# Preparing the experts' weights one matrix to a stretch, and counting taken tokens in f16

## The chip, the cores and the metric

One core of a Trainium2 chip runs the kernel. The time is that of the device for one execution, in microseconds, median over runs. The core's engines work side by side, each through its own instructions in order: PE (TensorE, with its weight loads shown as PEld), DVE (VectorE), ACT (ScalarE), POOL (GpSimd) and SP (SyncE, which here only starts transfers).

## The reference

Attention over 8 batches, 8 heads, 576 tokens, then a gated product of matrices, then a mixture of 8 experts in which every token goes to one expert. Scores are walked from the highest down, and an expert takes at most 576 tokens:

```python
logits = x @ w_gate
order = np.argsort(-logits.flatten())
for idx in order:
    tok, e = (int(idx) // E, int(idx) % E)
    if assigned[tok] >= 0 or counts[e] >= cap:
        continue
    assigned[tok] = e
    counts[e] += 1
for e in range(E):
    mask = assigned == e
    h = np.maximum(x[mask] @ w1[e], 0.0)
    out[mask] = h @ w2[e]
```

There are 4608 tokens of 512 values; `w1[e]` is 512 x 1024 and `w2[e]` is 1024 x 512, 2 MB each.

## The kernel before

The program goes through attention and the first matrices (to about 800 us), then a routing stage (about 857 to 1104 us), and then the experts, to the end.

**Routing.** `phase()` runs seven times, and in each it finds a threshold for every expert digit by digit, in nine levels: 63 levels in all. A level is a chain between PE and DVE. PE multiplies one-hot digits `T` with the masks `M` (p1, nine matmuls, L806); DVE makes `mk` (L821); PE sums it (p2, four matmuls, L827); DVE compares with the room left `R` to make `fl` (L830); PE sums `fl` with a constant matrix `q16` (p3, L832); DVE takes `dl` (L834), the mask `eq` (L840) and the next `M` (L789). Between p1 and `mk`, `taken` lowers `R` by the tokens that the level before has given out: a matmul of a constant `q32` with the counts `cnt`, both f32 (L796, shown as two instructions), and a subtraction on DVE (L797). Into the gaps of the chain `fill` puts a counted number of matmuls of another product: 2.4 behind p1, 2.2 behind p2, 5.2 behind p3. These come from `stream()`, which computes the rows of x (`px`, L966, 24 matmuls of 128x512 for each of 36 blocks) from `W34` and `g`; `g` is loaded by SP, split by ACT and corrected by an accumulating transfer of POOL (`gl`). PE, POOL and ACT are in hand-written order here; DVE's is the scheduler's.

**Preparing a weight matrix.** Each of the 16 matrices (`a` is `w1[e]`, `b` is `w2[e]`) is loaded by SP into a staging tile `esa` or `esb`, one buffer each (L1019); ACT takes the sums of squares in eight `red` steps (L1026, each with a read of the sum); `fin` adds them up on PE (L1031) and DVE makes a power of two from it; then eight `conv` steps write the scaled matrix as two f16 parts, the high one on ACT (L1040), the low one on DVE (L1041), into `ewa` or `ewb` (two buffers each). The ops of 0a, 0b and 1a (the number is the expert) are in the list `ew0`, from which `stream()` takes some after each block from its sixth on (L970 to L972). The converts of 0b and 1a are left out of that list and kept in `owed_w`.

**Experts.** They go in pairs, 0 to 3. A pair has four stretches: layer 1 of its first expert (units of 12 matmuls, L1121; ACT and DVE make `h`, L1123 and L1124), layer 2 on token blocks 0 to 3 (24 matmuls each, L1138; ACT makes `y`, L1141; POOL scatters it, L1143), layer 1 of the second expert, layer 2 on blocks 4 to 8. All of PE's results go through one psum pool `pe` of eight buffers. A unit is 128 or 192 tokens wide for expert 0 and 288 wide for the others. `gather(p)` fetches the tokens of a pair in nine blocks: an indirect transfer on POOL (L1092), a scale on DVE (L78 to L81), `x16` on ACT and DVE (L1096, L1097), a transposing transfer on SP (L1098). `interleave(a, b)` spreads the list b among the units of a; the scheduler may still move an instruction ahead where its inputs allow. Here b was: in layer 1 of the first expert, the second half of the second expert's weights (for pair 0 the converts in `owed_w`) in the first half of the units, and four gather blocks in the second; in blocks 0 to 3 the next pair's first `a` (in pair 0 after all of 1b); in layer 1 of the second expert five gather blocks; in blocks 5 to 8 the next pair's first `b` and second `a`.

Of the kernel before, what the change touches and what calls it, by code (L numbers as in the profile page):

```python
# [7 lines left out]
F32 = mybir.dt.float32  # L8
F32R = mybir.dt.float32r
F16 = mybir.dt.float16  # L10
BF16 = mybir.dt.bfloat16
I32 = mybir.dt.int32
AF = mybir.ActivationFunctionType
ALU = mybir.AluOpType
AX = mybir.AxisListType
# [6 lines left out]
DM, FF, E = 512, 1024, 8  # L22
# [23 lines left out]
def interleave(a, b):  # L46
    na, nb = len(a), len(b)
    ib = 0
    for ia, f in enumerate(a):
        f()  # L50
        while ib < nb and (ib + 1) * na <= (ia + 1) * nb:
            b[ib]()
            ib += 1
    while ib < nb:
        b[ib]()
        ib += 1
# [3 lines left out]
def moe_kernel(ctx, tc, q, k, v, moe_w1, moe_w2, moe_w3, moe_w_out, w_gate, ew1, ew2, out):  # L60
    nc = tc.nc
    P = 128
# [7 lines left out]
    ones = const.tile([P, P], F32, name="ones")  # L70
# [4 lines left out]
    def pow2(pool, m, name, TB=TB, **kw):  # L75
        n = m.shape[-1]
        t = pool.tile([P, 3, n], I32, name=name, **kw)
        nc.vector.tensor_scalar(t[:, 0], m.bitcast(I32), 24, 23, op0=ALU.logical_shift_right,  # L78
                                op1=ALU.logical_shift_left)
        nc.vector.tensor_scalar(t[:, 1], t[:, 0], -1.0, float((189 + TB) << 23), op0=ALU.mult, op1=ALU.add)  # L80
        nc.vector.tensor_scalar(t[:, 2], t[:, 0], float((65 - TB) << 23), None, op0=ALU.add)  # L81
        return t[:, 1].bitcast(F32), t[:, 2].bitcast(F32)
# [504 lines left out]
    for n, m in WSTEP.items():  # L587
        for _ in range(m):
            x = next(ws)
# [8 lines left out]
    for f in range(8):  # L598
        a, b_ = S3 + int(R3 * f), S3 + int(R3 * f + R3 / 2)
# [21 lines left out]
    first = {n0: g for g, (n0, n1) in enumerate(GROUPS)}  # L621
# [65 lines left out]
    nc.vector.tensor_copy(pf, pi)  # L687
    ones16 = rt.tile([P, P], F16, name="ones16")
    nc.gpsimd.memset(ones16, 1.0)
    q32 = rt.tile([P, P], F32, name="q32")  # L690
    nc.gpsimd.memset(q32, 0.25)
    ci = const_tile([P, P], F32, "ci", [[1, P]], 0, 0)
    ci4i = rt.tile([P, P], I32, name="ci4i")
    nc.gpsimd.iota(ci4i, pattern=[[1, P]], base=0, channel_multiplier=0)
# [52 lines left out]
    def phase():  # L747
# [45 lines left out]

        def taken(c):
            p4 = cwp["pr"].tile([P, E], F32, name="p4")
            nc.tensor.matmul(p4, q32, c, start=True, stop=True)  # L796
            nc.vector.tensor_tensor(out=R, in0=R, in1=p4, op=ALU.subtract)  # L797

        eq, A, owe = un, None, None
        for l in range(NL):  # L800
# [39 lines left out]
                nc.vector.scalar_tensor_tensor(eqn, d, dl, eq, op0=ALU.is_equal, op1=ALU.mult)  # L840
                Mn = M_of(eqn)
            with tc.issue_after(om[0].ins) if not last else ExitStack():
                cnt = rw.tile([P, E], F32, name="cnt")
                nc.vector.scalar_tensor_tensor(cnt, thr[:, 1 if last else 0], dl, p2, op0=ALU.is_equal, op1=ALU.mult)
                if l + 1 < 7 and TH < 9:
                    T_of(l + 1, TH, 9)
                nc.vector.scalar_tensor_tensor(ab, d, dl, eq, op0=ALU.is_ge if last else ALU.is_gt, op1=ALU.mult)
                if A is None:
                    A = ab
                    A_ = rw.tile(E36, F16, name="A")  # L850
                    nc.vector.tensor_copy(A_, ab)
                    A = A_
                else:
                    nc.vector.tensor_tensor(out=A, in0=A, in1=ab, op=ALU.add)
# [148 lines left out]
    EW = {}  # L1003
    ew0 = []
    cwp = {}

    owed_w = []

    def expert_w(e, part, width, early, late=False):
        nonlocal owed_w  # L1010
        cw = cwp["p"]
        ops = []
        for n, src, A_, N_, T in ((("a", ew1, 4, FF, 10), ("b", ew2, 8, DM, 15))[part],):
            k_ = 4096 // width
            d = {}

            def load(n=n, src=src, A_=A_, N_=N_, d=d):
                d["st"] = cw.tile([P, A_, N_], F32, name="es" + n)
                nc.sync.dma_start(d["st"], src[e].rearrange("(c p) f -> p c f", p=P))  # L1019
                d["m"] = cw.tile([P, 8], F32, name="em" + n, bufs=2)  # L1020
                d["w"] = cw.tile([P, 2, A_, N_], F16, name="ew" + n, bufs=2)
                d["s"] = d["st"].rearrange("p c f -> p (c f)")
                d["v"] = d["w"].rearrange("p z c f -> p z (c f)")

            def red(i, d=d):
                nc.scalar.activation(d["v"][:, 1, i * width:(i + 1) * width], d["s"][:, i * width:(i + 1) * width], AF.Square,  # L1026
                                     accum_out=d["m"][:, i:i + 1])

            def fin(n=n, T=T, d=d, k_=k_):
                m2 = cwp["ps"].tile([P, 512], F32, name="pe")  # L1030
                nc.tensor.matmul(m2[:, :k_], ones, d["m"][:, :k_], start=True, stop=True)  # L1031
                m3 = cw.tile([P, 1], F32, name="er" + n, bufs=2)
                nc.vector.tensor_reduce(m3, m2[:, :k_], axis=AX.X, op=ALU.add)
                d["sc"], i = pow2(cw, m3, "ep" + n, T, bufs=2)
                EW[e, n] = d["w"], i

            def conv(i, d=d):
                x = slice(i * width, (i + 1) * width)
                w, hi, lo = d["s"][:, x], d["v"][:, 0, x], d["v"][:, 1, x]
                nc.scalar.activation(hi, w, AF.Copy, scale=d["sc"])  # L1040
                nc.vector.scalar_tensor_tensor(lo, w, d["sc"], hi, op0=ALU.mult, op1=ALU.subtract)  # L1041

            ops.append(load)
            ops += [lambda i=i, f=red: f(i) for i in range(k_)]
            if early:
                ops += [lambda: None] * 3
            ops.append(fin)
            ops += [lambda i=i, f=conv: f(i) for i in range(k_)]
            if late:
                owed_w += ops[-k_:]  # L1050
                ops = ops[:-k_]
        return ops

    load_w34()
    prep_g(0)
# [8 lines left out]
    cwp["pr"] = pb.enter_context(tc.tile_pool(name="pr2", bufs=1, space=PSUM, reuse_waits="tile"))  # L1064
    cwp["ps"] = pb.enter_context(tc.tile_pool(name="pt", bufs=1, space=PSUM, reuse_waits="tile"))
    cwp["p"] = ctx.enter_context(tc.tile_pool(name="cw", bufs=1, side="right", reuse_waits="tile"))
    for x in range(3):
        ew0 += expert_w(x // 2, x % 2, 512, True, x > 0)
    ew0.pop(0)()

    with tc.manual_schedule(engines={mybir.EngineType.PE, mybir.EngineType.Pool, mybir.EngineType.Activation}):
        route()
# [73 lines left out]
            tc.declare_no_dep(d.ins, o.ins, reason="rows of other tokens")  # L1146
        scat.append(d)

    def weights(e, part):
        if (e, part) == (1, 1):  # L1150
            return owed_w
        return expert_w(e, part, 512, True) if 2 <= e < E else []

    for f in gather(0):
        f()
    for p_ in range(E // 2):
        e = 2 * p_
        more = gather(p_ + 1) if p_ + 1 < E // 2 else []
        first = [((0, P),), ((P, P),), ((2 * P, P),), ((3 * P, CAP - 3 * P),)]
        halves = [((0, 288), (288, 288))]  # L1160
        units = list(layer1(e, first if e == 0 else halves))
        interleave(units[:len(units) // 2], weights(e + 1, 1))
        interleave(units[len(units) // 2:], more[:4])
        interleave([lambda k_=k_: layer2(p_, k_) for k_ in range(4)],
                   (expert_w(1, 1, 512, True) if e == 0 else []) + weights(e + 2, 0))
        interleave(list(layer1(e + 1, halves)), more[4:])
        layer2(p_, 4)
        interleave([lambda k_=k_: layer2(p_, k_) for k_ in range(5, 9)], weights(e + 2, 1) + weights(e + 3, 0))


_INS = ['q', 'k', 'v', 'moe_w1', 'moe_w2', 'moe_w3', 'moe_w_out', 'moe2_w_gate', 'moe2_w1', 'moe2_w2']
# [33 lines left out]
```

## Time and profile before

| what | value |
|---|---|
| runs | 1553.21, 1556.84, 1563.21 us (median 1556.84) |
| profiled execution | 1554.94 us, span 1553.2 us |
| PE busy | 1370.7 us (88%) |
| PE weight loads | 933.2 us (60%) |
| DVE busy | 987.8 us (64%) |
| ACT busy | 947.5 us (61%) |
| POOL busy | 118.6 us (8%) |
| mean transfer rate | 167 GB/s |

Busy times are shares of the span of one execution. A matmul's duration in a row overlaps that of the next, so the distance of two starts tells what a matmul costs PE. A wait is the idle time of an engine just ahead of an instruction, put down to what came last.

### The profile page before, as it was taken

Reading aid. Unit: us, or ns where it says so; the run is one execution under the profiler, and the core shown is the slowest. Engines: PE = TensorE matmul, PEld = TensorE weight load, DVE = VectorE, ACT = ScalarE, POOL = GpSimd, SP = SyncE. Lnnn points to the kernel's source line nnn. Section 1 sums busy time; section 2 is a strip of 40 time slices with the busy share of each in tenths; the row PEclk is TensorE's granted clock in tenths of the full one; section 3 lists DMA queues with packets and bytes.
Section 4 is the critical chain, followed back from the end, with each engine's and each line's share of the span. In section 5 each row is a group of like instructions: output and inputs, shape, how many; then the busy total and the mean of one; then the engine's idle time right before and its main releaser. Section 6 shows DMA issues by size and latency. Waiting matters only on the chain. (4 is left out here: it accounts for less than half of the span.)

```text
span 1553.2 us, 32385 instructions
## 1 busy us (share of the span) xinstructions
PE 1370.7 (88%) x12622; PEld 933.2 (60%) x12622; DVE 987.8 (64%) x2986; ACT 947.5 (61%) x2213; POOL 118.6 (8%) x137
## 2 busy tenths in 40 slices
PE   4457887989899999989899999999589889899897
PEld 2335655666666666656567666666476456566663
DVE  8888989868987888785111777777666533632510
ACT  8879887767877777755233444664246754845521
POOL 0000000000000000010000110101142300110001
PEclk9667999999999999999999999999789989999999
DMA  7767896888767775649995877877395833621100
GB/s 260 175 160 180 188 239 147 170 157 180 209 150 187 174 163 124 120 97 261 270 298 140 247 195 204 197 192 178 119 220 185 204 122 102 184 95 62 68 28 35
DMA packets 385417, 259.52 MB, mean 167 GB/s; under 512 B 261872, under 2 KB 345328, under 8 KB 384240
## 3 DMA queue, kind: packets, MB, share of 16 engines
q1 hardware_dynamic: 372064, 215.47, 55.1%
q0 software_dynamic: 11520, 39.87, 11.0%
q8 instruction: 99, 1.62, 0.4%
q10 hardware_dynamic: 1680, 2.11, 0.4%
q14 instruction: 54, 0.44, 0.1%
HBM read 132.61 MB, written 39.86 MB: 111 GB/s over the span
## 5 line engine op out<-in xcount | busy, mean ns | idle before, releaser
L325 PE MATMUL ab<-xT,w1h 128*128 128x288 f16 x1536 | 222.5, 295 | 12.7 <-ACT a_sb L330 9.3
L325 PE MATMUL ab<-xT,w2h 128*128 128x288 f16 x1536 | 221.0, 294 | 3.8 <-DVE g L335 2.3
L1121 PE MATMUL pe<-xT,ewa 128*128 128x288 f16 (+2 forms) x1728 | 201.6, 282 | 14.9 <-DMA xT<-x 12.3
L1121 PEld LDWEIGHTS <-ewa 128*128 128x128 f16 x1728 | 162.6, 102 | 52.9 <-issue 15.2
L1138 PE MATMUL pe<-ewb,h 128*128 128x512 f16 (+1 forms) x960 | 189.1, 379 | 0.0
L325 PEld LDWEIGHTS <-w1h 128*128 128x128 f16 x1536 | 147.4, 101 | 64.6 <-issue 21.7
L245 ACT ACTIVATE E<-S,nb,cc 128x128 f32<-128x128 f32 (+4 forms) x288 | 181.5, 638 | 2.8 <-DVE P L256 1.0
L325 PEld LDWEIGHTS <-w2h 128*128 128x128 f16 x1536 | 148.5, 100 | 57.0 <-issue 14.0
L256 DVE SCALAR_TENSOR_TENSOR P<-E,rr,P 128x512 f16<-128x512 f32 (+4 forms) x288 | 156.0, 573 | 10.5 <-ACT P L255 10.1
L1138 PEld LDWEIGHTS <-h 128*128 128x128 f16 (+1 forms) x960 | 85.4, 101 | 99.1 <-issue 2.6
L300 PE MATMUL PV<-PT,v 128*64 128x128 f16 (+1 forms) x2880 | 100.9, 222 | 48.4 <-DMA PT<-P 28.3
L1124 DVE SCALAR_TENSOR_TENSOR h<-pe,h 128x288 f16<-128x288 f32 (+2 forms) x144 | 58.9, 420 | 113.3 <-ACT h L1123 113.3
L300 PEld LDWEIGHTS <-v 128*64 128x64 f16 x2880 | 83.8, 117 | 73.4 <-issue 35.6
L335 DVE SCALAR_TENSOR_TENSOR g<-ab,vr,a_sb 128x288 f32<-128x288 f32 x124 | 63.4, 512 | 99.3 <-PE ab L325 84.5
L966 PE MATMUL px<-W34h,gl 128*128 128x512 f32 x288 | 120.2, 418 | 1.3 <-DMA gl<-g 1.3
L966 PE MATMUL px<-W34h,gh 128*128 128x512 f32 x288 | 120.9, 420 | 0.0
L966 PE MATMUL px<-W34l,gh 128*128 128x512 f32 x288 | 120.4, 418 | 0.0
L255 ACT ACTIVATE P<-E,rr 128x128 f16<-128x128 f32 (+3 forms) x176 | 97.3, 604 | 22.9 <-DVE rr L249 13.6
L237 DVE TENSOR_REDUCE nb<-S 128x2 f32<-128x1024 f32 (+3 forms) x128 | 101.5, 813 | 5.1 <-PE S L228 5.0
L1123 ACT ACTIVATE h<-pe 128x288 f16<-128x288 f32 (+2 forms) x144 | 51.5, 378 | 87.0 <-PE pe L1121 87.0
L330 ACT ACTIVATE a_sb<-ab 128x288 f32<-128x288 f32 x128 | 52.1, 407 | 71.6 <-PE ab L325 71.5
L224 PE MATMUL S<-qkT 64*128 64x512 f16 (+3 forms) x768 | 78.6, 317 | 12.6 <-ACT E L245 12.6
(285 smaller groups left out, 2199.9 us busy)
## 6 DMA issues: line engine op xcount, KB each, us to landing
g<-gd SPq DMA_DIRECT2D x36, 512.0 KB, 5.1
gl<-g POOLq DMA_DIRECT2D x36, 512.0 KB, 6.1
gd<-g SPq DMA_DIRECT2D x62, 288.0 KB, 3.3
g<-gd SPq DMA_DIRECT2D x15, 1152.0 KB, 8.0
raw<-in_moe_w_dram SPq DMA_DIRECT2D x32, 512.0 KB, 4.4
esa<-in_moe_w_dram SPq DMA_DIRECT2D x8, 2048.0 KB, 8.9
esb<-in_moe_w_dram SPq DMA_DIRECT2D x8, 2048.0 KB, 9.4
v<-in_v_dram SPq DMA_DIRECT2D x8, 1280.0 KB, 6.3
```

The costliest lines, as they stand in the source:

```text
L224: nc.tensor.matmul(ps[:, hh, o:o + N], tq[r, a, m * P:m * P + P], tk[r, b, :N], start=a + b == 0, stop=False)
L237: nc.vector.tensor_reduce(nb[:, 0, k_:k_ + 2], ps[:, :, o:o + N], axis=AX.X, op=ALU.max)
L245: nc.scalar.activation(ef[:, a], pf_[:, a], AF.Exp, bias=nb[:, 1, x:x + 1], scale=c[:, 0:1], accum_out=sums[:, x:x + 1])
L255: nc.scalar.activation(hi, ef[:, at[x]], AF.Copy, scale=r[:, 1, x:x + 1])
L256: nc.vector.scalar_tensor_tensor(lo, ef[:, at[x]], r[:, 1, x:x + 1], hi, op0=ALU.mult, op1=ALU.subtract)
L300: nc.tensor.matmul(ps[hh * 64:hh * 64 + 64, c0:c0 + w], vt[:, zv, hh, j, :], s, start=z == 0 and j == 0, stop=z == 2 and j == nj - 1)
L325: nc.tensor.matmul(p[:, :288], w[:, zw, cc, :], x[:, zx, cc, c0:c0 + 288], start=first, stop=cc == 3 and zw == 1)
L335: nc.vector.scalar_tensor_tensor(g, ps["w2"][:, :288], iv[b][:, f:f + 1], a, op0=ALU.mult, op1=ALU.mult)
L966: nc.tensor.matmul(p, gh[a][:, f], W34[b][:, f], start=f == 0 and a + b == 0, stop=f == 7 and a == 1)
L1121: nc.tensor.matmul(p[:, :n], w1[:, a, cc, f * P:(f + 1) * P], t[:, 4 * b + cc, x], start=cc == 0 and a + b == 0, stop=cc == 3 and a == 1)
L1124: nc.vector.scalar_tensor_tensor(h[:, 1, f, x], p[:, :n], 0.0, h[:, 0, f, x], op0=ALU.max, op1=ALU.subtract)
L1138: nc.tensor.matmul(p[r0:r1], h[:, a, f, k_ * P + r0:k_ * P + r1], EW[e, "b"][0][:, b, f], start=f == 0 and a + b == 0, stop=f == 7 and a == 1)
```

## The change

The counts `cnt` are written in f16, and `taken` multiplies them with `q16`, the f16 constant that p3 uses already; `q32` and its memset go. Each matrix x = 2e + part is now a pair of a load and a list of ops in `mats`, and `phase_of(x, units, rows)` deals one matrix to one stretch: the load of the next matrix, x + 1, then the ops of matrix x, with the gather blocks put in at even distances, all spread over the stretch's units. Pair p's four stretches prepare the second expert's a and b, and the next pair's first a and b; gather blocks go 3, 2, 3 and 1 to the four. In the routing stage both loads of expert 0 are issued ahead, and `ew0` holds the ops of 0a, the load of 1a, and all ops of 0b with its converts.

```diff
-            nc.tensor.matmul(p4, q32, c, start=True, stop=True)
+            nc.tensor.matmul(p4, q16, c, start=True, stop=True)
...
-                cnt = rw.tile([P, E], F32, name="cnt")
+                cnt = rw.tile([P, E], F16, name="cnt")
...
-    owed_w = []
-
-    def expert_w(e, part, width, early, late=False):
...
+    def expert_w(e, part):
+        cw = cwp["p"]
+        n, src, A_, N_, T = (("a", ew1, 4, FF, 10), ("b", ew2, 8, DM, 15))[part]
+        width, k_ = 512, 8
+        d = {}
+
+        def load():
+            d["st"] = cw.tile([P, A_, N_], F32, name="es" + n)
+            nc.sync.dma_start(d["st"], src[e].rearrange("(c p) f -> p c f", p=P))
+
+        def red(i):
+            if i == 0:
+                d["m"] = cw.tile([P, 8], F32, name="em" + n, bufs=2)
+                d["w"] = cw.tile([P, 2, A_, N_], F16, name="ew" + n, bufs=2)
...
+        return load, ([lambda i=i: red(i) for i in range(k_)] + [lambda: None] * 3 + [fin]
+                      + [lambda i=i: conv(i) for i in range(k_)])
+
+    mats = [(lambda: None, [])] * (2 * E + 3)
...
-    for x in range(3):
-        ew0 += expert_w(x // 2, x % 2, 512, True, x > 0)
-    ew0.pop(0)()
+    for x in range(2 * E):
+        mats[x] = expert_w(x // 2, x % 2)
+    mats[0][0]()
+    mats[1][0]()
+    ew0 += mats[0][1] + [mats[2][0]] + mats[1][1]
...
-    def weights(e, part):
-        if (e, part) == (1, 1):
-            return owed_w
-        return expert_w(e, part, 512, True) if 2 <= e < E else []
+    def phase_of(x, units, rows):
+        load, ops = mats[x + 1][0], mats[x][1]
+        ops = [load] + ops
+        for i, f in enumerate(rows):
+            ops.insert((2 * i + 1) * len(ops) // (2 * len(rows)), f)
+        interleave(units, ops)
...
-        units = list(layer1(e, first if e == 0 else halves))
-        interleave(units[:len(units) // 2], weights(e + 1, 1))
-        interleave(units[len(units) // 2:], more[:4])
-        interleave([lambda k_=k_: layer2(p_, k_) for k_ in range(4)],
-                   (expert_w(1, 1, 512, True) if e == 0 else []) + weights(e + 2, 0))
-        interleave(list(layer1(e + 1, halves)), more[4:])
-        layer2(p_, 4)
-        interleave([lambda k_=k_: layer2(p_, k_) for k_ in range(5, 9)], weights(e + 2, 1) + weights(e + 3, 0))
+        phase_of(2 * e + 2, list(layer1(e, first if e == 0 else halves)), more[:3])
+        phase_of(2 * e + 3, [lambda k_=k_: layer2(p_, k_) for k_ in range(4)], more[3:5])
+        phase_of(2 * e + 4, list(layer1(e + 1, halves)), more[5:8])
+        phase_of(2 * e + 5, [lambda k_=k_: layer2(p_, k_) for k_ in range(4, 9)], more[8:])
```

DVE in the routing stage, at the converts of 0b, before the change (`ewb` is written by the low half of a convert; `mk`, `fl`, `dl`, `eq`, `M` are the level's chain):

```order
L1041 SCALAR_TENSOR_TENSOR ewb<-esb,epb,ewb 128x512
L821 TENSOR_TENSOR mk<-p_15260,delta 128x32
L721 TENSOR_TENSOR T<-dp,iok 128x640
L797 TENSOR_TENSOR R<-R,p_15270 128x8
L1041 SCALAR_TENSOR_TENSOR ewb<-esb,epb,ewb 128x512 x2
L830 SCALAR_TENSOR_TENSOR fl<-R,p_15279 128x8
L1041 SCALAR_TENSOR_TENSOR ewb<-esb,epb,ewb 128x512 x2
L834 TENSOR_REDUCE dl<-p_15288 128x1
L1041 SCALAR_TENSOR_TENSOR ewb<-esb,epb,ewb 128x512 x2
L840 SCALAR_TENSOR_TENSOR eq<-dp,dl,eq 128x36
L1041 SCALAR_TENSOR_TENSOR ewb<-esb,epb,ewb 128x512
L789 TENSOR_TENSOR M<-oh,eq 128x288
```

The same place after the change:

```order
L819 TENSOR_TENSOR mk<-p_15691,delta 128x32
L795 TENSOR_TENSOR R<-R,p_15701 128x8
L719 TENSOR_TENSOR T<-dp,iok 128x640
L1036 SCALAR_TENSOR_TENSOR ewb<-esb,epb,ewb 128x512
L828 SCALAR_TENSOR_TENSOR fl<-R,p_15711 128x8
L832 TENSOR_REDUCE dl<-p_15720 128x1
L838 SCALAR_TENSOR_TENSOR eq<-dp,dl,eq 128x36
L787 TENSOR_TENSOR M<-oh,eq 128x288
```

The eight converts stood in one level and R behind T; now there is one in a level, and R stands ahead of T.

ACT at the start of pair 1, before (`h` is layer 1's result; `ewb,emb<-esb` is a red of a b matrix, the wide rows are converts):

```order
L1123 ACTIVATE h<-pe 128x288 x2
L1026 ACTIVATE ewb,emb<-esb 128x512 x5
L1123 ACTIVATE h<-pe 128x288
L1026 ACTIVATE ewb,emb<-esb 128x512
L1123 ACTIVATE h<-pe 128x288
L1026 ACTIVATE ewb,emb<-esb 128x512 x2
L1123 ACTIVATE h<-pe 128x288
L1040 ACTIVATE ewb<-esb,epb 128x512 x8
```

After, at the same place (x_ rows are gather blocks):

```order
L1132 ACTIVATE y<-pe,s_16878 128x512
L1114 ACTIVATE h<-pe 128x288
L1087 ACTIVATE x_19399<-xg,xsc 128x512
L1114 ACTIVATE h<-pe 128x288 x2
L1087 ACTIVATE x_19512<-xg,xsc 128x512
L1114 ACTIVATE h<-pe 128x288 x3
L1021 ACTIVATE ewb,emb<-esb 128x512 x8
L1114 ACTIVATE h<-pe 128x288 x5
L1035 ACTIVATE ewa<-esa,epa 128x512 x8
L1114 ACTIVATE h<-pe 128x288 x5
```

The reds of a b matrix stood behind two units, and its fin on PE behind five; now they stand behind six units, and the convert among the units is that of an a matrix, whose reds ran earlier.

DVE in layer 1 of expert 0 (`xsc` and `x_` rows are gather blocks), before:

```order
L1097 SCALAR_TENSOR_TENSOR x_17691<-xg,xsc,x_17691 128x512
L1099 COPY sc<-xsc 128x1
L1124 SCALAR_TENSOR_TENSOR h<-pe,h 128x128
L1097 SCALAR_TENSOR_TENSOR x_17747<-xg,xsc,x_17747 128x512
L1124 SCALAR_TENSOR_TENSOR h<-pe,h 128x128
L78 TENSOR_SCALAR xsc<-xg 128x1
L1124 SCALAR_TENSOR_TENSOR h<-pe,h 128x192
L80 TENSOR_SCALAR xsc<-xsc 128x1
```

After, about the same place:

```order
L1036 SCALAR_TENSOR_TENSOR ewa<-esa,epa,ewa 128x512
L1090 COPY sc<-xsc 128x1
L1036 SCALAR_TENSOR_TENSOR ewa<-esa,epa,ewa 128x512
L78 TENSOR_SCALAR xsc<-xg 128x1
L1036 SCALAR_TENSOR_TENSOR ewa<-esa,epa,ewa 128x512
L1115 SCALAR_TENSOR_TENSOR h<-pe,h 128x128
L1036 SCALAR_TENSOR_TENSOR ewa<-esa,epa,ewa 128x512
L80 TENSOR_SCALAR xsc<-xsc 128x1
L81 TENSOR_SCALAR xsc<-xsc 128x1
L1036 SCALAR_TENSOR_TENSOR ewa<-esa,epa,ewa 128x512
L1088 SCALAR_TENSOR_TENSOR x_17657<-xg,xsc,x_17657 128x512
L1090 COPY sc<-xsc 128x1
```

The low halves of 1a's converts now stand among the `h` of this stretch; before there were none.

## Rows read from the trace of the kernel before

**Rows 1.** Windows of the trace: stretch, us, busy (instructions) of PE, PEld, DVE, ACT, POOL, clock, DMA share, GB/s

```profile
857.00:1104.00 247.00, 236.29 (x1738) 164.56 (x1737) 179.50 (x819) 125.85 (x237) 25.86 (x30) 0.98 0.78 199
1128.60:1158.70 30.10, 27.36 (x384) 27.27 (x385) 19.66 (x94) 14.72 (x42) 13.72 (x13) 0.88 1.15 218
1229.70:1339.90 110.20, 97.30 (x636) 61.03 (x635) 48.01 (x122) 62.14 (x145) 14.22 (x14) 0.94 0.46 136
1339.90:1442.10 102.20, 97.50 (x636) 61.09 (x635) 38.90 (x84) 57.67 (x137) 9.04 (x9) 0.97 0.30 106
```

**Rows 2.** Timeline of PE in routing: start us, us, engine, line, operation, count.

```profile
1060.49 0.39 PE L806 MATMUL p<-M,Tc 128*128 128x32 f16 x9
1060.73 0.37 PE L796 MATMUL p<-cnt,q 128*128 128x8 f32 x2
1060.95 0.48 PE L966 MATMUL px<-W34h,gl 128*128 128x512 f32 x1
...
1062.39 0.18 PE L832 MATMUL p<-fl,q 128*128 128x8 f16 x1
1062.43 0.47 PE L966 MATMUL px<-W34l,gh 128*128 128x512 f32 x1
...
1063.67 0.28 PE L796 MATMUL p<-cnt,q 128*128 128x8 f32 x2
1063.80 0.47 PE L966 MATMUL px<-W34h,gh 128*128 128x512 f32 x1
```

**Rows 3.** Windows of PE's px matmuls (L966) alone: stretch, us, busy (count), clock, DMA.

```profile
970.00:1005.00 35.00, 31.74 (x115) 1.00 0.81 193
1006.16:1014.51 8.35, 4.02 (x10) 0.80 0.66 168
1087.88:1098.42 10.54, 6.40 (x15) 0.68 0.51 143
```

**Rows 4.** Timeline of PE in the first clump of converts; in brackets idle before, releaser.

```profile
1008.06 0.24 PE L827 MATMUL p<-mk,selk 128*128 128x8 f16 x4 [1.50 <-DVE mk L821]
...
1013.71 0.29 PE L806 MATMUL p<-M,T 128*128 128x32 f16 x5 [0.84 <-DVE M L789]
```

**Rows 5.** Waits of DVE, 857 to 1104: us in total, times, longest.

```profile
DVE dl L834 <- PE p L832: 25.8, 56, 0.7
DVE fl L830 <- PE p L827: 24.3, 51, 2.3
```

**Rows 6.** Waits of PE, 870 to 960: the same columns.

```profile
PE p L806 <- DVE M L789: 1.9, 3, 0.8
PE px L966 <- DMA gl<-g: 1.3, 1, 1.3
```

**Rows 7.** Waits of PE in the experts, 1128 to 1554.

```profile
PE pe L1031 <- ACT ewb L1026: 22.1, 3, 12.9
...
PE pe L1121 <- DVE h L1124: 2.7, 1, 2.7
```

**Rows 8.** Timeline of PE at the end of pair 0 and starts of pairs 1 and 3.

```profile
1219.19 10.52 PE L1138 MATMUL pe<-ewb,h 128*128 128x512 f16 x48
...
1229.69 7.51 PE L1121 MATMUL pe<-xT,ewa 128*128 128x288 f16 x60
...
1250.55 18.73 PE L1121 MATMUL pe<-xT,ewa 128*128 128x288 f16 x132
...
1454.57 19.11 PE L1121 MATMUL pe<-xT,ewa 128*128 128x288 f16 x132
```

**Rows 9.** Timeline of SP's queue and ACT at the start of pair 1.

```profile
1232.66 0.37 SPq L1019 DMA_DIRECT2D esb<-in_moe_w_dram  x1
...
1244.46 0.63 ACT L1026 ACTIVATE ewb<-esb 128x512 f16<-128x512 f32 x1 [4.41 <-DMA esb<-in_moe_w_dram]
```

**Rows 10.** Tile esb (and ewb): operation, count, ns min/median/max; landing of its loads.

```profile
L1041 DVE SCALAR_TENSOR_TENSOR ewb<-esb,epb,ewb x64: 734/746/761, 1007.2 to 1460.7; 128x512 f16<-128x512 f32 x64
...
DMA to landing us min/median/max: 8.6/9.4/19.8
```

More of the change, by code (lines that the diff above doesn't have):

```diff
@@ L689, in moe_kernel @@
     nc.gpsimd.memset(ones16, 1.0)
-    q32 = rt.tile([P, P], F32, name="q32")
-    nc.gpsimd.memset(q32, 0.25)
     ci = const_tile([P, P], F32, "ci", [[1, P]], 0, 0)
@@ L1005, in moe_kernel @@
     cwp = {}
-    owed_w = []
-    def expert_w(e, part, width, early, late=False):
-        nonlocal owed_w
+    def expert_w(e, part):
         cw = cwp["p"]
[L1012 to L1019, printed above, removed]
+        n, src, A_, N_, T = (("a", ew1, 4, FF, 10), ("b", ew2, 8, DM, 15))[part]
[6 more added lines that the diff above has]
+            if i == 0:
                 d["m"] = cw.tile([P, 8], F32, name="em" + n, bufs=2)
@@ L1023, in load @@
                 d["v"] = d["w"].rearrange("p z c f -> p z (c f)")
[L1025 to L1052, printed above, removed]
+            nc.scalar.activation(d["v"][:, 1, i * width:(i + 1) * width], d["s"][:, i * width:(i + 1) * width], AF.Square,
+                                 accum_out=d["m"][:, i:i + 1])
+        def fin():
+            m2 = cwp["ps"].tile([P, 512], F32, name="pe")
+            nc.tensor.matmul(m2[:, :k_], ones, d["m"][:, :k_], start=True, stop=True)
+            m3 = cw.tile([P, 1], F32, name="er" + n, bufs=2)
+            nc.vector.tensor_reduce(m3, m2[:, :k_], axis=AX.X, op=ALU.add)
+            d["sc"], i = pow2(cw, m3, "ep" + n, T, bufs=2)
+            EW[e, n] = d["w"], i
@@ new lines, in conv @@
+        def conv(i):
+            x = slice(i * width, (i + 1) * width)
+            w, hi, lo = d["s"][:, x], d["v"][:, 0, x], d["v"][:, 1, x]
+            nc.scalar.activation(hi, w, AF.Copy, scale=d["sc"])
+            nc.vector.scalar_tensor_tensor(lo, w, d["sc"], hi, op0=ALU.mult, op1=ALU.subtract)
+        return load, ([lambda i=i: red(i) for i in range(k_)] + [lambda: None] * 3 + [fin]
+                      + [lambda i=i: conv(i) for i in range(k_)])
+    mats = [(lambda: None, [])] * (2 * E + 3)
```

## Prediction

> **What bounds the kernel now.** I read the engine table and the slices of the page first: PE is busy 88% of the span, so a change pays only where PE waits, where its clock falls or where it does less. Then I cut the second half into windows [rows 1]. In the routing stage PE is busy 236.29 of 247.00 us: the counted matmuls of `stream()` fill what the routing leaves. The experts are PE's too, with holes: the first unit group, 1128.60 to 1158.70, holds 2.7 us, and pair 1 (1229.70 to 1339.90) has PE busy for 97.30 of 110.20 us, where pair 2, with the same 636 matmuls, takes 102.20. PE's waits in the experts [rows 7] name the holes: 22.1 us in three waits at L1031 (the fin matmul of a "b" matrix), the longest 12.9, and 2.7 us for a DVE `h`. The other two share 9.2 us; they stand at the starts of pairs 2 and 3. After each hole PE also runs slower: 132 matmuls take 18.73 us after the first and 19.11 after the last, and at the rate of the 60 just ahead (7.51 us) they would take 16.5 [rows 8].
>
> **The sum**, against the profiled 1554.94 us (1.9 under the median 1556.84, well inside the 10 us by which the runs differ).
>
> *Counts in f16.* In a steady level the f32 pair of L796 starts at 1060.73 and the next px at 1060.95, 0.22 us [rows 2]. The f16 matmul of the same shape (L832, also followed by a px) occupies 1062.39 to 1062.43, 0.04 us. The px behind either goes on to its successor alike, so I credit 0.18 us in the 56 levels in which `taken` follows p1. In the seven last levels the pair stands between px and takes 0.13 (1063.67 to 1063.80), so 0.09 each. 56 x 0.18 + 7 x 0.09 = **-10.7**. Nine f16 matmuls with nine weight loads take 0.24 us at L806, 0.027 each, so the bound below is -11.4; a bound above comes under the rivals, where the gain doesn't reach the end. Does it reach it? DVE's chain must keep up with a PE that comes 0.18 us sooner. DVE waits for PE before fl 51 times, 24.3 us, and before dl 56 times, 25.8 us [rows 5]: some 0.9 us of slack in a level. R moves ahead of T on DVE, which it can, since its matmul now ends sooner. So it does, by most of it.
>
> The Trainium skill (TensorE: Matmul & The Clock Gate, LDWEIGHTS (loading the stationary operand)) puts a load at its columns divided by 1.2, in ns, for 128 columns an estimate of 107. If every load showed, the saving would be one load in a level, 63 x 0.11 = 7 us, and the sum 4 us higher. The nine loads within 0.24 us say that they don't show.
>
> *Clumps gone.* The 16 owed converts of 0b and 1a were dealt to the first half of L1(0), but the scheduler issued each set of eight as one clump on DVE in the routing stage. There mk and M come late, 1.50 and 0.84 us in the first [rows 4], and the clock falls to 0.80 and 0.68 [rows 3]. In the undisturbed stretch PE issues 115 px in 35.00 us, 3.29 per us [rows 3]. The first clump's 8.35 us hold 10 px (3.04 us worth), the second's 10.54 hold 15 (4.57): 5.3 + 6.0 = **-11.3**. In exchange the converts of 0b now come one per stream step. The nearest row is 0a, converted in four pairs: three M waits, 1.9 us, about 0.5 a pair [rows 6]. A single (0.746 us, [rows 10]) is half a pair: 8 x 0.25 = **+2** (0 to 4).
>
> *Stream sooner.* PE eats the stream faster, while SP, ACT and POOL still make each gl in their own time with the same buffers. Before, PE waited for gl once, 1.3 us [rows 6]. I add **+2** (0 to 4): one or two more such waits.
>
> *1a's converts in L1(0).* They move into the first unit group: eight on ACT, and eight on DVE around one `h`. DVE is busy 19.66 of 30.10 us there, and 8 x 0.746 = 6.0 us are added in a lump [rows 1, 10]. Units are about 1 us and psum holds eight, which covers a delay of that size only if DVE was up to date; before it was not, by 2.7 us [rows 7]. So 0 (all covered) to 9 (6.0 + 2.7); I take **+4**.
>
> *The three holes at pair starts.* Why was the first 12.9? Load b was issued at 1232.66, after L1(2) had begun at 1229.69, and ACT's first red ran at 1244.46 [rows 8, 9]: 11.8 us, then eight reds, and the fin stands in PE's order only five units (7.51 us) into L1. After the change the matrix whose fin stands in the first stretch of a pair is an "a" matrix, loaded a stretch ahead and reduced in the blocks before. So all three fin waits go, 22.1 us, and with them the slow clock, 2.2, about 2.4 and 2.6 [rows 8]: **-29.3**.
>
> What is late next? The b matrix, one stretch on. Its staging tile is single, so its load waits until the last stretch's eight b converts are done on DVE. Those follow the fin behind block 7, take 8 x 0.746 = 6 us, and one block (half of the 48 matmuls in 10.52 us, [rows 8], so 5 us) is left: the load is issued some 3 us into the next L1. As at 1232.66, 11.8 us later the reds can start, about 15 us in. On ACT they now stand behind five or six `h`, ready by 9 us, and in front of all other `h`. ACT is thus stopped from 9 to 15 and reduces until 21 or 22 (eight times 0.63 and the read of the sum). PE needs the seventh `h` only when psum's eight buffers are used: at unit 14 or 15, 20 to 21 us in. So the wait ends within a microsecond or two of the need, on either side. Bounds: nothing (covered), or 8 us a pair (a landing some 5 us later, with the clock loss of the rows 2 to 2.6). I take 4, of which about 2 is clock: 3 x 4 = **+12** (0 to 24).
>
> Edits at nothing: the moved gather rows. Each block's x16 must only be there a pair later, and POOL's gathers stand behind scatters whose `y` is ready. If that cover goes, ACT waits at an x16 and `y` behind it is late, and psum covers as above. The ninth gather now stands behind the sixth block's scatter, with two blocks, the same 10.52 us, to spare.
>
> Sum: -10.7 - 11.3 + 2 + 2 + 4 - 29.3 + 12 = -31.3, so 1554.94 - 31.3 = **1523.6**, said as 1524. All terms at their good ends: -11.4 - 11.3 - 29.3 = -52, 1503; all at their bad ends: -10.7 - 11.3 + 4 + 4 + 9 - 29.3 + 24 = -10.3, 1545. Ends do not all meet, so 1510 to 1541.
>
> **Rivals.**
>
> *No hole left.* The b load lands in time and L1(0) covers its converts: 1523.6 - 12 - 4 = 1508. For it: the margin above is about even. Against: after every hole of before PE was slow for a while, and any remaining wait brings that back.
>
> *The experts gain nothing.* ACT, stopped at a red with the `h` behind it, takes over as the hole: 8 us at each of three starts and 9 in L1(0) eat the 29.3. 1554.94 - 10.7 - 11.3 + 4 = 1537, up to 1541. For it: ACT works in order, and what fin waited for before, the b load, is still issued when the pair starts.
>
> *The f16 gain stays inside the level.* If DVE's chain sets the level's length in the stretches with converts, PE just waits for fl or M sooner. No gain there: 1523.6 + 10.7 = 1534; with the experts' rival as well 1548, the same time as before. Against it are the waits of [rows 5].
>
> *Slower.* Loads of 2 MB now run beside gathers, scatters and transposes in every stretch. If they land late, ACT stops at the reds with `h` and `y` behind it. One mechanism, at the three pair starts: from about 15 us into L1 each us of further delay is a us of PE. To go 1% above the median (1572.4) from 1523.6 it takes 49 us, 16 at each start, so landings of about 28 us instead of 11.8. The longest landing of a b load was 19.8, the median 9.4 [rows 10], with the DMA share between 0.30 and 0.46 in the pairs [rows 1]. So it is unlikely.
>
> The Trainium skill (DMA: Bandwidth & Descriptors, Issuing engines are not separate DMA queues) says that transfers started by SP and POOL run on the same 16 engines and interleave, which speaks against loading beside gathers. The trace shows room in the pairs, but not in the first unit group, where the DMA share reads 1.15.
>
> **How the numbers follow.** Forecast (1510 to 1541 with its sizes as bounded) 0.62; no hole left 0.12; the experts gain nothing 0.11; the f16 gain stays inside the level 0.10 (half of it with the experts' rival); slower 0.05. About 1% is what a measurement of this kernel can tell from no change: faster is under 1541.3, slower above 1572.4. Faster: 0.62 + 0.12 + most of 0.11 + half of 0.10, less what the bad ends of the terms take, is 0.84; same 0.11; slower 0.05. The range is 1508 to 1541: it takes in the hole-free case and the experts' rival and leaves about 2 in 10 out.
>
> **What would show it.** The routing stage shorter by 15 to 20 us; L796's line with half its matmuls and about 0.04 us each in the timeline; no waits of PE for mk, fl or M over 0.8 us. In PE's waits no 12.9 us at the fin line, but possibly waits for `h` or for ACT in the first stretch of pairs 1 to 3, a few us each; pair 1 about 102 us long, near pair 2 of before. L1(0) longer by some us, with a wait of its matmuls for DVE `h`. Wrong would be: PE waits for fl or dl's chain in each level (the f16 term fails), ACT idle for "DMA esb" over 8 us at a pair's start with PE waiting for `h` at once (the +12 fails), or x16 rows of ACT waiting for POOL's gathers with `y` behind them.

## The result, and the profile after

The changed kernel takes 1533.81 us, the median of four runs (1529.2 to 1536.92), beside 1556.92 for the kernel before (four runs): a ratio of 0.984, 95% interval 0.981 to 0.987. Measured once more beside the experiments it was 0.978 (0.973 to 0.984). It is faster by 23 us where 33 were forecast (1556.84 to 1524); 1533.81 lies inside the range. The profiled execution took 1529.2 us, 25.7 less than that of before.

Where the 25.7 us came from is read off PE's timeline. The table gives stretches of it, each from its first matmul to the first one of the next stretch (routing: from the start of the first p1 matmul to that of the last px), for this and for the experiments below:

| kernel | ratio to before | routing | layer 1, expert 0 | blocks 0 to 3 behind it | layer 1 at the start of pairs 1, 2, 3 |
|---|---|---|---|---|---|
| before | 1 | 254.2 | 30.1 | 21.0 | 39.4, 31.4, 31.4 |
| changed | 0.984 | 234.1 | 35.8 | 23.2 | 39.8, 25.5, 23.7 |
| e1 f16 alone | 0.988 | 243.0 | 27.4 | 21.0 | 38.5, 31.9, 31.4 |
| e2 deal alone | 0.988 | 244.7 | 41.1 | 22.1 | 34.7, 28.2, 23.7 |
| e3 1a in the stream | 0.978 | 243.5 | 29.0 | 20.9 | 38.4, 25.6, 23.7 |
| e4 gathers held on POOL | 0.971 | 237.6 | 31.5 | 20.9 | 23.7, 25.6, 23.7 |
| e5 before, gathers held | 0.992 | 258.4 | 28.9 | 21.0 | 30.0, 31.0, 31.1 |
| e6 as e4, loads in halves | 0.978 | 242.4 | 27.8 | 20.9 | 25.4, 27.4, 23.7 |
| e7 gathers held on DVE | 0.966 | 236.9 | 27.7 | 20.9 | 23.7, 23.8, 23.7 |
| e8 loads in halves | 0.981 | 246.9 | 42.3 | 22.2 | 30.6, 23.7, 23.7 |
| e9 as e7, idle gathers | 0.960 | 237.1 | 29.2 | 20.9 | 24.0, 27.9, 23.7 |
| e10 changed again | 0.978 | 235.2 | 36.0 | 22.4 | 32.4, 25.7, 23.7 |

All other stretches of the experts agree within 1 us, except in e6 (27.9, 27.9 and 26.5 against 23.8 in layer 1 of the second experts) and for the blocks 0 to 3 of pairs 1 and 2 in e4 (22 against 20.9). In the changed kernel routing gave 20 us, pairs 2 and 3 gave 13.6, and layer 1 of expert 0 with the blocks behind it took 8 back. Pair 1 gave nothing. Each stretch is read from one execution. Routing has the same instructions in e5 as in the kernel before and reads 258.4 against 254.2, and the changed kernel's reads 234.1 to 237.6 in five kernels that share it (changed, e4, e7, e9, e10), so a stage is good to some 4 us.

Windows of the changed kernel (columns as in [rows 1]): layer 1 of expert 0, pair 1, pair 2.

```profile
1108.10:1144.00 35.90, 27.85 (x387) 26.68 (x388) 25.15 (x108) 21.03 (x54) 11.29 (x12) 0.88 1.08 190
...
1217.00:1327.70 110.70, 98.54 (x635) 61.06 (x633) 47.47 (x139) 63.54 (x149) 17.42 (x17) 0.95 0.58 145
1327.70:1424.00 96.30, 94.59 (x634) 59.65 (x633) 41.28 (x92) 60.27 (x145) 10.30 (x10) 1.00 0.38 122
```

Pair 1 is 110.7 us, as long as before, though DVE has the same work; pair 2 is 96.3 where it was 102.2. PE's waits in the experts say what replaced the fin:

```profile
PE pe L1112 <- DVE h L1115: 19.9, 5, 6.9
PE pe L1112 <- DMA xT<-x: 12.4, 1, 12.4
```

The 22.1 us at the fin line of [rows 7] are gone, and PE waits 19.9 us for `h` on DVE instead. The level in routing looks like this (PE's timeline, as [rows 2]):

```profile
1079.97 0.39 PE L804 MATMUL p<-M,Tc 128*128 128x32 f16 x9
1080.21 0.17 PE L794 MATMUL p<-cnt,q 128*128 128x8 f16 x1
1080.24 0.47 PE L964 MATMUL px<-W34h,gl 128*128 128x512 f32 x1
```

From the start of L794 to the px it is 0.03 us now, where the f32 pair took 0.22. PE's waits in routing after the change (us in total, times, longest):

```profile
PE p L804 <- DVE M L787: 2.1, 5, 0.8
PE px L964 <- DMA gl<-g: 1.4, 1, 1.4
PE p L825 <- DVE mk L819: 1.3, 3, 0.7
```

In pair 1 the reader can follow the hole back through four engines. PE's timeline first:

```profile
1217.08 5.45 PE L1112 MATMUL pe<-xT,ewa 128*128 128x288 f16 x42
1222.97 6.78 PE L1112 MATMUL pe<-xT,ewa 128*128 128x288 f16 x54 [0.43 <-issue]
1234.56 4.52 PE L1112 MATMUL pe<-xT,ewa 128*128 128x288 f16 x24 [4.81 <-DVE h L1115]
...
1250.54 6.52 PE L1112 MATMUL pe<-xT,ewa 128*128 128x288 f16 x36 [6.92 <-DVE h L1115]
```

Both holes are put down to `h`. DVE's timeline in the same place:

```profile
1224.57 2.07 DVE L1036 SCALAR_TENSOR_TENSOR ewb<-esb,epb,ewb 128x512 f16<-128x512 f32 x3
1231.15 0.15 DVE L78 TENSOR_SCALAR xsc<-xg 128x1 int32<-128x1 int32 x1 [4.52 <-DMA xg<-xr,idx]
1231.22 1.41 DVE L1036 SCALAR_TENSOR_TENSOR ewb<-esb,epb,ewb 128x512 f16<-128x512 f32 x2
...
1250.03 0.46 DVE L1115 SCALAR_TENSOR_TENSOR h<-pe,h 128x288 f16<-128x288 f32 x1 [11.73 <-ACT h L1114]
```

DVE stands 4.52 us at the scale (L78) of a gathered block that has not landed, and behind that one small instruction wait the last two converts of b and every `h`. Scales and gathers both come in the order of the blocks, and this scale is the 30th of 36; POOL had issued the 30th gather 13.4 us earlier:

```profile
1217.80 0.96 POOL L1083 DMA_INDIRECT xg<-xr,idx  x1 [0.30 <-issue]
```

SP's queue and ACT show the rest:

```profile
1232.66 0.37 SPq L1013 DMA_DIRECT2D esb<-in_moe_w_dram  x1
```

```profile
1232.78 0.72 ACT L1087 ACTIVATE x<-xg,xsc 128x512 f16<-128x512 f32 x1 [6.50 <-DVE xsc L81]
...
1244.70 0.63 ACT L1021 ACTIVATE ewb<-esb 128x512 f16<-128x512 f32 x1 [7.41 <-DMA esb<-in_moe_w_dram]
```

Load b goes out at 1232.66, when the last convert has read its staging tile, 15.6 us into the pair (from 1217.08). ACT waits 6.5 us for the scale, with `h` behind it too, and after a few `h` another 7.4 for the load, until 27.6 us into the pair. From its issue to the first red the load took 12.0 us, where it was 11.8 before: it is not slow, it is issued late.

### The profile page after: what moved, and what is told of

Read it like the earlier page. It is cut to its first block, busy times and chain, and to the rows that moved or that the text cites. A ratio compares the mean times of both kernels' runs of the same rounds, so it can differ in the third digit from the quotient of the medians.

```text
span 1527.5 us, 32254 instructions
## 1 busy us (share of the span) xinstructions
PE 1351.0 (88%) x12559; PEld 914.7 (60%) x12559; DVE 982.1 (64%) x2986; ACT 944.0 (62%) x2213; POOL 116.9 (8%) x136
## 5 line engine op out<-in xcount | busy, mean ns | idle before, releaser
L325 PE MATMUL ab<-xT,w1h 128*128 128x288 f16 x1536 | 218.8, 292 | 13.5 <-ACT a_sb L330 10.5
L1112 PE MATMUL pe<-xT,ewa 128*128 128x288 f16 (+2 forms) x1728 | 198.4, 278 | 33.2 <-DVE h L1115 19.9
L1112 PEld LDWEIGHTS <-ewa 128*128 128x128 f16 x1728 | 159.3, 100 | 71.3 <-issue 35.1
L224 PE MATMUL S<-qkT 64*128 64x512 f16 (+3 forms) x768 | 79.8, 321 | 12.9 <-ACT E L245 12.8
## 6 DMA issues: line engine op xcount, KB each, us to landing
esb<-in_moe_w_dram SPq DMA_DIRECT2D x8, 2048.0 KB, 12.1
```

Of the source, the lines that this page charges most:

```text
L224: nc.tensor.matmul(ps[:, hh, o:o + N], tq[r, a, m * P:m * P + P], tk[r, b, :N], start=a + b == 0, stop=False)
L325: nc.tensor.matmul(p[:, :288], w[:, zw, cc, :], x[:, zx, cc, c0:c0 + 288], start=first, stop=cc == 3 and zw == 1)
L1112: nc.tensor.matmul(p[:, :n], w1[:, a, cc, f * P:(f + 1) * P], t[:, 4 * b + cc, x], start=cc == 0 and a + b == 0, stop=cc == 3 and a == 1)
```

## The experiments

**The f16 counts alone (e1).** The kernel before with

```diff
-            nc.tensor.matmul(p4, q32, c, start=True, stop=True)
+            nc.tensor.matmul(p4, q16, c, start=True, stop=True)
...
-                cnt = rw.tile([P, E], F32, name="cnt")
+                cnt = rw.tile([P, E], F16, name="cnt")
```

> The kernel before with the counts in f16 and nothing else. The forecast's term says -10.7 us against the kernel before (56 levels by 0.18 and 7 by 0.09 us), so about 1546, with px waits in the clumps as before or a little longer. Rival: DVE's chain sets the level's length, the gain stays inside, and the time is that of the kernel before within 3 us, with more PE waits for fl and M.

Ratio 0.988 (0.983 to 0.993), 18 us of 1561.5, with an interval of 11 to 26 us, and 10.7 lies just below it. The stage is the sharper measure: 254.2 to 243.0 us, -11.2. The rival falls. The experts keep their holes, as they should:

```profile
PE pe L1029 <- ACT ewb L1024: 23.9, 3, 12.4
```

**The deal alone (e2).** The changed kernel with `q32` and an f32 `cnt` back.

> The changed kernel with the counts in f32 as before, so the new deal alone. If the two parts add up it is 10 to 11 us slower than the changed kernel, about 1544, and the routing stage is about 11 us longer than in the changed kernel, with the experts as in the changed kernel (110.7 us for pair 1). Rival: the deal frees slack on DVE that the f16 part needs; then this kernel with f32 loses less than 7 us to the changed one, or the kernel with f16 alone gains less than 7.

Ratio 0.988 (0.984 to 0.992), median 1544.78 beside 1561.5. Routing is 244.7 us, 10.6 more than in the changed kernel and 9.5 less than before: 11.2 and 9.5 add up to 20.7, and the changed kernel gained 20.1. Within the 4 us of a stage the two parts don't lean on each other. In the experts the expectation missed: layer 1 of expert 0 took 41.1 and that of pair 1 34.7 us, not the 35.8 and 39.8 of the changed kernel. The sizes of these holes differ between executions of the changed kernel itself (e10 below); that it is the landing of the gathers that differs is not shown for e2.

**1a's converts in the stream (e3).**

```diff
-    ew0 += mats[0][1] + [mats[2][0]] + mats[1][1]
+    ew0 += mats[0][1] + [mats[2][0]] + mats[1][1] + mats[2][1]
+    mats[2] = (mats[2][0], [])
```

> The changed kernel with the eight converts of 1a (and all its other steps) in the stream list instead of layer 1 of expert 0. Theory converts: the 35.9 us of that stretch (30.1 before) come from the eight converts on DVE, so it falls to about 30 and the routing stage gains 2 us: total -4 us against the changed kernel. Theory gather: the stretch is long because DVE stands at the scale of a gathered block that has not landed (3.2 us, with the h behind it); the gathers are still in it, so it stays at 33 or more and the total within 2 us of the changed kernel. Pair 1 is as in the changed kernel, about 110, by both.

Layer 1 of expert 0 falls to 29.0 and the blocks behind it to 20.9, which is what the theory of the converts says; but the stream gave back 9.4 us, not gained 2 (243.5 against 234.1), since the scheduler now put the converts there in pairs (PE waits for `M` 5.5 us in routing, against 2.1, which is part of the 9.4). The ratio, 0.978 (0.973 to 0.983), is that of the changed kernel measured again. Pair 1's two holes are in place:

```profile
1235.66 5.92 PE L1113 MATMUL pe<-xT,ewa 128*128 128x288 f16 x24 [4.63 <-DVE h L1116]
...
1250.99 6.67 PE L1113 MATMUL pe<-xT,ewa 128*128 128x288 f16 x36 [4.77 <-DVE h L1116]
```

**Gathers held on POOL (e4).** Each dealt gather is queued behind the last scatter written:

```diff
+        def held(f):
+            def g():
+                with tc.issue_after(scat[-1].ins) if scat else ExitStack():
+                    f()
+            return g
...
-            ops.insert((2 * i + 1) * len(ops) // (2 * len(rows)), f)
+            ops.insert((2 * i + 1) * len(ops) // (2 * len(rows)), held(f))
```

> The changed kernel with each gather held on POOL behind the last scatter issued so far, so that blocks of a later pair are gathered in the stretch they are dealt to and not a pair ahead. Theory gather: in the changed kernel DVE stops at the scale of a late block (4.5 us at the end of pair 0) with b converts and h behind it, and so the next b load is issued late; here the converts run in one piece, load b is issued about 3 us into pair 1, the hole of 4.8 us goes and that of 6.9 falls to 2 or less: pair 1 about 98 us, and layer 1 of expert 0 about 31: total -12 to -17 us against the changed kernel. Theory load: the holes come from load b's own landing (12 us from its issue behind the converts) and from the lump of converts, whatever the gathers do: pair 1 stays above 106, the total within 5 us of the changed kernel.

Ratio 0.971 (0.966 to 0.977): some 20 us under the changed kernel by its first ratio, some 11 by its second (12 to 17 were expected). Pair 1's layer 1 is 23.7 us without a hole, where it was 39.8; the theory of the gathers holds there. Layer 1 of expert 0 was 31.5 us, as expected, but not free. What is left of PE's waits:

```profile
PE pe L1112 <- DMA xT<-x: 12.4, 1, 12.4
PE pe L1112 <- DVE h L1115: 5.0, 4, 2.5
...
PE pe L1129 <- ACT h L1114: 2.0, 2, 1.1
```

**The kernel before, gathers held (e5).** The same edit on `more` of the kernel before.

> The kernel before with each gather held on POOL behind the last scatter issued so far, the old deal of weights kept. If the holes at the pair starts were made by the old deal (a fin five units into the pair that waits for a b matrix loaded only when the pair begins), they stay: 20 us or more of PE waits at the fin line, and the time within 6 us of the kernel before (a few us less, since the load no longer queues behind all nine transposes). If pulled-ahead gathers alone made them, as in the changed kernel's pair 1, the fin waits fall under 8 us and the kernel is 12 us or more faster than before.

Between the two: ratio 0.992 (0.989 to 0.995), 10 to 13 us.

```profile
PE pe L1031 <- ACT ewb L1026: 13.5, 3, 4.7
```

The fin waits fall from 22.1 to 13.5, nearly all of it at pair 1, whose layer 1 goes from 39.4 to 30.0; pairs 2 and 3 keep theirs (31.0, 31.1). So of the 12.9 us hole of before, about 8 were the gathers' already, and the old deal owned 4 to 5 at each of three starts, with PE's slower matmuls behind them. How the gathers made that hole can be read as well. Before, DVE took the sums of b only 4.4 us after PE had them (its fin ended at 1219.33), behind the scales and low halves of late blocks, and stood at one more before the first convert; so load b went out 3.0 us into the pair [rows 8, 9]:

```profile
1218.98 0.15 DVE L78 TENSOR_SCALAR xsc<-xg 128x1 int32<-128x1 int32 x1 [3.27 <-DMA xg<-xr,idx]
...
1223.74 0.15 DVE L1033 TENSOR_REDUCE erb<-pe 128x1 f32<-128x8 f32 x1
...
1226.75 0.15 DVE L78 TENSOR_SCALAR xsc<-xg 128x1 int32<-128x1 int32 x1 [1.93 <-DMA xg<-xr,idx]
```

With the gathers held (e5) it goes out 3.6 us ahead of the pair, which starts at 1235.89:

```profile
1232.32 0.37 SPq L1019 DMA_DIRECT2D esb<-in_moe_w_dram  x1
```

**Loads in halves (e6 on e4, e8 on the changed kernel).** Each staging tile becomes two of half the size, each with a load:

```diff
-            d["st"] = cw.tile([P, A_, N_], F32, name="es" + n)
-            nc.sync.dma_start(d["st"], src[e].rearrange("(c p) f -> p c f", p=P))
+            d["st"] = [cw.tile([P, A_ // 2, N_], F32, name=f"es{n}{z}") for z in range(2)]
+            for z in range(2):
+                nc.sync.dma_start(d["st"][z], src[e].rearrange("(c p) f -> p c f", p=P)[:, z * A_ // 2:(z + 1) * A_ // 2])
...
```

> The kernel with held gathers, with each staging tile cut in two halves of 1 MB with a load of its own, so that the first half of a matrix is loaded when four converts of the one before are done, not eight. Theory: the wait left at the start of pair 2 (1.4 us for h, layer 1 of its first expert 25.6 against 23.7) is the single b load's, so it goes: layer 1 at all pair starts 23.6 to 24, total 2 to 4 us under the kernel with held gathers (1518). Rival: that wait is ACT's order (reds in front of h) and not the load; then it stays and the total is the same.

> The changed kernel with the staging tiles in halves and the gathers left as they are. The first half of b is loaded after four converts, which in the changed kernel's trace were done before DVE stood at the late gather. Theory: the first hole of pair 1 (4.8 us, h behind the stop) stays and the second (6.9 us, reds waiting for b) shrinks by 4 us or more: layer 1 there about 33 to 36 instead of 39.8; total 4 to 8 us under the changed kernel. Rival, the load is late for the traffic of the gathers: both holes stay.

Both missed on the total. With the halves the scheduler laid the gathers and converts out anew. In e6 (0.978 beside e4's 0.971, intervals that overlap) PE waits 9.4 us in layer 1 for the scales of gathers, in stretches that had none before:

```profile
PE pe L1114 <- DVE xsc L80: 9.4, 5, 2.4
```

In e8 (0.981) layer 1 of pair 1 was 30.6 instead of 39.8, more gained than expected, but layer 1 of expert 0 went to 42.3 and routing to 246.9. About half of what routing lost in e8, and all that it lost in e6 against e4, is one more stop of the same kind: a half load goes out as soon as four converts are done, ACT stands at a red that waits for it (9.9 us in e8, 8.8 in e6), and behind the red stands the next convert's high half, for which DVE waits with `M` behind it (PE waits for that `M` 6.3 and 5.7 us). The edit changes too much at once to tell load from gathers, and it shows only that the second hole can shrink.

**DVE's part of the gathers held (e7).** As e4, but held behind the last low half of a convert, which binds DVE alone:

```diff
-            nc.vector.scalar_tensor_tensor(lo, w, d["sc"], hi, op0=ALU.mult, op1=ALU.subtract)
+            last_cv[0] = nc.vector.scalar_tensor_tensor(lo, w, d["sc"], hi, op0=ALU.mult, op1=ALU.subtract)
...
+                with tc.issue_after(last_cv[0].ins) if last_cv[0] is not None else ExitStack():
+                    f()
```

> The changed kernel with the DVE part of each gather block (scale and low half) held behind the last convert written so far on DVE; POOL may still gather as early as its four buffers allow. If the stop of DVE at a late block's scale is what made the holes of pair 1, this is as good as holding the gathers themselves: layer 1 of pair 1's first expert 24 to 27 us instead of 39.8, total 12 us or more under the changed kernel. If the gathers' own traffic and POOL's order made b late, it stays above 32 us there, and the total within 6 us of the changed kernel.

Ratio 0.966 (0.960 to 0.972), median 1508.12: with e9, the fastest of the kernels here, and the theory of the DVE stop holds. PE runs pair 1's layer 1 in one piece (PE, DVE, SP and ACT of the same stretch):

```profile
1206.98 14.86 PE L1113 MATMUL pe<-xT,ewa 128*128 128x288 f16 x120
...
1221.82 8.98 PE L1113 MATMUL pe<-xT,ewa 128*128 128x288 f16 x72
```

```profile
1203.31 5.39 DVE L1036 SCALAR_TENSOR_TENSOR ewb<-esb,epb,ewb 128x512 f16<-128x512 f32 x8 [0.17 <-ACT ewb L1035]
```

```profile
1208.73 0.37 SPq L1013 DMA_DIRECT2D esb<-in_moe_w_dram  x1
```

```profile
1219.62 0.63 ACT L1021 ACTIVATE ewb<-esb 128x512 f16<-128x512 f32 x1 [4.68 <-DMA esb<-in_moe_w_dram]
```

The eight converts run in 5.39 us without a stop, the load goes out 1.75 us into the pair, and ACT's reds start at 12.6 us. Layer 1 of expert 0 is 27.7 with the same eight converts of 1a on DVE: by themselves they cost nothing. Two things are not told apart here: the late block stopped ACT too (6.5 us at its x16, with `h` behind), and e7 takes both stops away, so the share of ACT's in the first hole of pair 1 is not shown. The late issue of load b, and with it the second hole, is DVE's.

**Is it the traffic? (e9).** e7 with five gathers more, held on POOL behind blocks 5 to 7 of pairs 0 and 1, into a tile that nobody reads. The tile has one buffer, so POOL waits for each to land and only one is under way at a time.

> The kernel whose DVE part of the gathers is held, with five more gathers in the last stretch of pairs 0 and 1, where the changed kernel has its pulled-ahead ones; they read rows that nobody uses, so no engine waits for them and only POOL and the transfer engines see them. Theory DVE stop: the holes of pair 1 come from DVE standing at a late scale, so nothing changes: layer 1 at the start of pair 1 stays 24 to 25 us, the load of b is issued 2 to 3 us into the pair, and the total is within 4 us of 1508. Theory traffic: the gathers' transfers make b late, so the b load lands 3 us or more later than 11.5 and layer 1 there is 28 us or more.

In pair 1 nothing happens (24.0), and the ratio, 0.960 (0.954 to 0.965), is no worse than e7's. In pair 2 layer 1 takes 27.9:

```profile
1308.74 0.37 SPq L1013 DMA_DIRECT2D esb<-in_moe_w_dram  x1
```

```profile
1321.23 0.63 ACT L1021 ACTIVATE ewb<-esb 128x512 f16<-128x512 f32 x1 [7.68 <-DMA esb<-in_moe_w_dram]
```

```profile
1327.38 6.24 PE L1113 MATMUL pe<-xT,ewa 128*128 128x288 f16 x36 [2.34 <-DVE h L1116]
```

There the load goes out 3.2 us into the pair (from 1305.59) and ACT's reds start at 15.6, 12.5 us after the issue; PE then waits 2.34 us and loses another 1.7 in the slower matmuls behind. ACT had begun the converts 1.4 us later than in pair 1 of e7, and there the reds started 10.9 us after the issue. So the traffic of gathers one at a time is not what makes the 16 us of pair 1. Four at a time, as the changed kernel has them, were not tried; but its own load b took 12.0 us, no longer than here. Still, the margin is thin enough for a microsecond or two to show; how much of pair 2's 4 us is traffic and how much the later converts stays open. Why the gathers land late is not shown either.

**The changed kernel again (e10).**

> The changed kernel as it is, beside the others on the same chip: 0.984 of the kernel before, and the holes in the same places, 4 to 7 us each in layer 1 at the start of pair 1, 2 us in pair 2, none in pair 3, if they come from the program's order and not from one execution.

```profile
1244.76 6.29 PE L1112 MATMUL pe<-xT,ewa 128*128 128x288 f16 x36 [6.70 <-DVE h L1115]
```

The second hole is there again, the first is not (load b went out at 1227.65, 9.2 us into the pair and not 15.6): layer 1 of pair 1 was 32.4, that of pair 2 25.7, of pair 3 23.7. The place is the program's, the size the execution's.

## Why the prediction was right or wrong, step by step

**Counts in f16: right.** The term was -10.7 in the profile's sum; alone it took 11.2 out of routing (e1) and, taken back, gave 10.6 (e2). The row that decided, 0.04 us for the f16 matmul, was 0.03 at the new place, so the weight load behind the matmul does not show, and the sum by the Trainium skill's figure (TensorE: Matmul & The Clock Gate, LDWEIGHTS (loading the stationary operand)), 4 us higher, lies farther from both than the forecast. The slack in DVE's chain was as read: DVE waits for fl's sum 31 times and 14.5 us now, where it was 51 and 24.3 [rows 5], and still for dl's 56 times.

**Clumps, singles, sooner stream: right.** -11.3 + 2 + 2 = -7.3 was forecast, -9.5 measured (e2). PE's longest wait for `mk` is 0.7 us now and for `M` 0.8, where [rows 4] had 1.50 and 0.84 in one clump. PE waits for gl once, 1.4 us, as before, so the +2 for the stream was not paid in that execution; with the same routing e10, e4, e7 and e9 wait 2.3 to 3.9 us, so it was paid in part there.

**1a's converts: inside the bounds, wrong cause.** The forecast took +4 (0 to 9) for a lump of 6 us on DVE. Measured were +5.7 in the stretch and +2.2 in the blocks behind it, 7.9 and twice the +4. But e7 has the same converts and the stretch takes 27.7, and e3, without them but with gathers between the `h`, 29.0. It is converts and gathers together that cost: DVE stood at a late gather's scale with six converts and the `h` behind it.

```profile
1137.56 0.15 DVE L78 TENSOR_SCALAR xsc<-xg 128x1 int32<-128x1 int32 x1 [3.20 <-DMA xg<-xr,idx]
```

```profile
1140.87 2.08 PE L1112 MATMUL pe<-xT,ewa 128*128 128x192 f16 x12 [4.90 <-DVE h L1115]
```

**The three holes: the step that failed is "edits at nothing: the moved gather rows".** The fin waits and their slow clock went as forecast (-29.3, and pair 3 gained all of its 7.7). The next bottleneck, the b load that is issued when the eight converts are done and stops ACT, was read rightly, and so was its threshold: reds about 15 us into the pair cost PE nothing to 2 us. They started at 12.6 in e7 (no hole), at 15.3 in pair 2 of the changed kernel (hole 1.7 and no more) and at 15.6 in e9 (hole 2.3):

```profile
1342.95 0.63 ACT L1021 ACTIVATE ewb<-esb 128x512 f16<-128x512 f32 x1 [5.84 <-DMA esb<-in_moe_w_dram]
```

Wrong was when the load goes out: "some 3 us into the next L1", because the converts would take 6 us in one piece. It went out 15.6 us into pair 1, 5.8 into pair 2 and 1.8 into pair 3. The term of +12 was then 4 too high in pair 3, 2 too high in pair 2, and 12 too low in pair 1, where it came to 16. What was missed there is that the scheduler runs gathers a pair and more ahead, as far as their buffers let it: the five that POOL issues from 1212.37 to 1220.38 are the last block of pair 2 and four of pair 3, and they land between pair 0's last converts. The kernel before did this too (seven gathers of pairs 2 and 3 from 1210.45 to 1227.53), so its trace could have told. The prediction looked at ACT's x16 and POOL's scatters for a late block, gave the ninth gather "the same 10.52 us, to spare", and never asked what stands behind a block's first instruction on DVE. The x16 rows of ACT that it named as a sign of being wrong did wait, 6.5 us, with `h` behind them. Some 8 us of the hole of before were the gathers' as well (e5), where the prediction put all 12.9 down to the old deal.

That the sum came so near is in part luck. Against the rows, routing and the old holes gave some 4 us more than forecast (20.1 and 31.1 against 18 and 29.3), and the new holes and layer 1 of expert 0 took some 10 more (17.9 and 7.9 against 12 and 4). The 16 us of pair 1 are twice the bound of 8 for a pair, and the total stayed inside the range because pairs 2 and 3 paid next to nothing; in e10 pair 1 paid 8.7.

**The rivals.** "No hole left" is what e7 reached with the gathers out of the way: 0.966 of before, where 1508 would be 0.969. "The experts gain nothing" was true of pair 1 alone, and by ACT and DVE together. "The f16 gain stays inside" fell with e1. "Slower" did not come: b loads landed in 12.1 us at the median, where it was 9.4, and at the three pair starts ACT's first red ran 12.0, 9.5 and 9.7 us after the issue, far from 28. The Trainium skill's rule is that transfers of all queues interleave on the same 16 engines (DMA: Bandwidth & Descriptors, Issuing engines are not separate DMA queues); no run here ties the shift of 2.7 us in the median to it, since e3, with its gathers ahead as well, has 9.4, and e7, with them held, 11.5.

## What to carry to other kernels

A small instruction that waits for a transfer can cost far more than its own wait, through what is queued behind it on its engine (4.5 us on DVE here, 16 in the pair): before a list of transfers is dealt anew, look in the order of each engine for what stands behind the first use of each block, not only for where the transfer is issued. When work is spread "evenly", look at where the scheduler really puts it; a queue dependence in one place (e7, nothing but an order on DVE) gave 1.3 to 1.9% on top (ratios taken on different chips), about as much as the whole change. And when one hole is taken away, ask of the old hole too whether it had one cause or two, by removing the suspected one alone (e5).

## What the runs showed that was not expected

A gathered block of 128 rows by 513 values landed up to 13.4 us after its issue when scatters, transposes and other gathers ran beside it (issue 1217.80, use 1231.15, DVE waiting for it); the longest landing in the profile of before was 8.2. Holding gathers on DVE alone held them on POOL too, through their four buffers, so that it left no gather between the last five scatters of a pair. And halving the loads, an edit of nothing but size, moved routing by 5 to 13 us (237.6 to 242.4 on e4, 234.1 to 246.9 on the changed kernel), through one red of ACT that stood at its load in e6, and about half through it in e8.
